# Causal attention with a decay bias, then a hard-swish MLP: a new hand order for the first eight head pairs and the first MLP block

## The chip, the cores and the metric

The kernel runs on one core of a Trainium2 chip. The metric is device time in microseconds (us) of one execution, the median over several. Engines are named as in the profile: PE (TensorE, matmul), PEld (its weight loads), DVE (VectorE), ACT (ScalarE), POOL (GpSimd), SP (SyncE, which here only issues transfers).

## The reference

There are 8 x 8 = 64 heads with 576 positions and 64 columns. Each head computes causal softmax attention with a bias that falls with the running sum of `max(s, 0)`. The 4608 x 512 result goes through an MLP with 2048 hidden columns.

```python
scores = scale * np.matmul(q, k.transpose(0, 1, 3, 2))
cum = np.cumsum(np.maximum(s, 0.0), axis=-1)
bias = -(cum[:, :, :, None] - cum[:, :, None, :])
scores = np.where(causal, -1000000000.0, scores + np.minimum(bias, 0.0))
attn = np.exp(scores - np.max(scores, axis=-1, keepdims=True))
attn = attn / (np.sum(attn, axis=-1, keepdims=True) + 1e-09)
x = np.matmul(attn, v)              # heads side by side: 4608 x 512
h = x @ w_in                        # 512 x 2048
g = h * np.clip(h + 3.0, 0.0, 6.0) / 6.0
out = g @ w_out                     # 2048 x 512
```

## The kernel before, in words

Heads are worked in 32 pairs. For a pair, `load_qk` and `load_v` bring q, k and v in float32 from HBM on SP's queue: two transfers for q and k, three for v. `cast_qk` (POOL) and `cast_v` (DVE for pairs 1 to 4, else POOL) make them float16. For the first ten pairs `transpose_group` turns q and k on TensorE in two groups, of five and four tiles of 128 x 128, and DVE copies the result into one of three slots of `qkT`; later pairs are transposed by DMA. Rows 64 to 127 of a slot hold the bias and a part of the causal mask: `mask_rows` fills them for each of the three slots, and for the first ten pairs `load_aug` writes the four rows of the running sum (three of it in float16 pieces for k, its negative for q) over the first of them. These rows are computed on DVE and ACT at the start, stored to HBM (`kaug_scratch`, `qaug_scratch`) and read back per pair; those of pair 0 are copied directly.

`scores_bank` computes one of four banks of a head's scores on TensorE, ACT takes the exponential into `Pm`, POOL zeroes what lies above the diagonal (the mask, L295). `attend` multiplies by the values (15 matmuls of 65 columns, the 65th gives the sum), and after the second head of a pair DVE takes the reciprocal and the product. `x_transpose` turns the pair's result into `xT`, on TensorE or by DMA.

The MLP works in nine blocks of 512 rows. `m1(n, f)` is four matmuls of 512 columns into a bank, then ACT (`trl`) and DVE (`gT`); there are 16 of them in a block. `m2(n, t4, part)` is four of the sixteen matmuls of an output tile; there are 16 parts in a block too. Such four matmuls are called a group here. Four pairs (one batch entry) give 576 rows of x, so block 0 needs the first four pairs. The weights w_in (two halves) and w_out (four parts) are loaded and cast by transfers that POOL issues, `load_w_in` and `load_w_out`.

PSUM has eight banks: tag M with two (`bank()`), S with three (scores, some transposes), Y with one (m2's output), O with two (attend).

There is no scheduler: the order on each engine is the order of the Python calls. `att_tasks(p)` gives the attention tasks of pair p with costs, `weave` puts MLP tasks between attention tasks in proportion to the costs, and `merged` mixes m1 of one block with m2 of the block before. In before, pairs 0 to 3 and the scores of pair 4 run first without MLP work (`att_of[0]`). Then m1 of block 0 and eight of its m2 parts are woven with pairs 4 to 8, m1 of block 1 with the other eight, two m1 to one m2, and from block 2 on 16 m1 with 16 m2 of the block before. SP's queue is in order, too: a transfer that waits holds all behind it.

The buffers that order the loads: `qkf` (float32 q and k) has three, v, `qkT` and `Pm` have three slots each.

Of the kernel before, what the change touches and what calls it, by code (L numbers as in the profile page):

```python
# [9 lines left out]
F32 = mybir.dt.float32  # L10
# [6 lines left out]
def kernel(  # L17
# [53 lines left out]
    kaug_dram = nc.dram_tensor("kaug_scratch", (3, NH * SEQ), F16, kind="Internal").ap()  # L71
    qaug_dram = nc.dram_tensor("qaug_scratch", (1, NH * SEQ), F16, kind="Internal").ap()
# [36 lines left out]
    kaug = work.tile([NH, 3, SEQ], F16, tag="s3", bufs=1)  # L109
    qaug = work.tile([NH, SEQ], F16, tag="s4", bufs=1)  # L110
# [8 lines left out]
    nc.gpsimd.memset(warm, 0.0)  # L119
# [16 lines left out]
    def load_qk(p, eng):  # L136
        b, h0 = (2 * p) // H, (2 * p) % H
        t = work.tile([128, NTR, 2, D], F32, tag="qkf", bufs=3, name=f"qkf{p}")
        for i, src in enumerate((q, k)):
            rows = src[b, h0:h0 + 2].rearrange("h s d -> (h s) d")  # L140
            eng.dma_start(  # L141
                out=t[:, :, i, :], in_=rows.rearrange("(t p) d -> p t d", p=128)
            )
        qk_f[p] = t
# [14 lines left out]
    def load_aug(p, eng):  # L159
        sl = p % NS  # L160
        c0 = p * W2
        eng.dma_start(out=kT[64:67, sl, 0:W2], in_=kaug_dram[:, c0:c0 + W2])
        eng.dma_start(out=qT[67:68, sl, 0:W2], in_=qaug_dram[:, c0:c0 + W2])
# [62 lines left out]
    def cast_v(p):  # L226
        sl = p % NS
        copy = nc.vector.tensor_copy if p in (1, 2, 3, 4) else nc.gpsimd.tensor_copy
        copy(out=v_h[:, sl, :, :, 0:D], in_=v_f[:, sl])  # L229
# [12 lines left out]
    def transpose_group(p, g):  # L242
        t0, t1 = ((0, 5), (5, 9))[g]
        n = (t1 - t0) * 128
        pT = half_bank(p < 5)
# [157 lines left out]
    def m1(n, f):  # L403
        if f == 0:
            gT[n] = work.tile([128, NF, 512], F16, tag="gT", bufs=2, name=f"gT{n}")
        ph = bank()
# [14 lines left out]
    def m2(n, t4, part):  # L421
        if part == 0:

            if (n, t4) in ((0, 1), (8, 1), (8, 3)):
                pouts[n, t4] = bank()
            else:
                pouts[n, t4] = psum.tile([128, 512], F32, tag="Y", name=f"po{n}_{t4}")
# [28 lines left out]
    load_v(0, nc.sync)  # L456
# [8 lines left out]
    for hh in range(2):  # L465
# [3 lines left out]
    nc.sync.dma_start(  # L469
        out=kaug_dram.rearrange("r (h t) -> h r t", h=NH), in_=kaug  # L470
    )
    nc.sync.dma_start(out=qaug_dram.rearrange("r (h t) -> h (r t)", h=NH), in_=qaug)
    mask_rows(1, nc.scalar.copy)
    load_v(1, nc.sync)
    load_aug(1, nc.sync)
    load_qk(2, nc.sync)
    load_v(2, nc.sync)

    weights_at = {1: [(load_w_in, 0)], 2: [(load_w_in, 1)]}
    pairs_at = {0: [3], 1: [4], 2: [], 3: [5], 4: [6], 5: [7, 8]}  # L480

    def att_tasks(p):
# [4 lines left out]
        def loads():  # L487
            if p + 2 < PTD:
                load_aug(p + 2, nc.sync)
            if p == 5:  # L490
                load_columns()
            for m in pairs_at.get(p, [p + 3] if p + 3 < NP else []):
                load_qk(m, nc.sync)
                load_v(m, nc.sync)
            if 4 < p < PTD - 1:
                cast_qk(p + 1)

        def casts():
            if more:
                cast_v(p + 1)  # L500
            if p + 2 <= 4:
                cast_qk(p + 2)
            if PTD <= p + 2 < NP:
                cast_columns(p + 2)
                transpose_dma(p + 2)
            for load, c in weights_at.get(p, []):
                load(c)

        def scores(hd):
            return [(lambda bi=bi: scores_bank(hd, bi), 400) for bi in range(4)]  # L510
# [5 lines left out]
        here = tr if p != 4 else [[], []]  # L516
        late = [(lambda: attend(2 * p - 1), 1200)] if p > 0 else []
        back = [(lambda: x_transpose(p - 1), 0 if by_dma(p - 1) else 640)] if p > 0 else []
        a = [(loads, 0)]
        if p <= PXD:  # L520
            a += scores(2 * p) + here[0] + late
            a += scores(2 * p + 1) + [(casts, 0)] + here[1] + back
        else:
            s0, s1 = scores(2 * p), scores(2 * p + 1)
            a = late + (back + a if by_dma(p - 1) else a + s0[:2] + back)
            a += (s0 if by_dma(p - 1) else s0[2:]) + here[0]
            a += s1 + [(casts, 0)] + here[1]
        if p == 6:
            a += [(decay_columns, 640)]
        if p == 7:  # L530
            a += [(copy_columns, 0)]
        c = [(lambda: attend(2 * p), 1200)]
        if p == 4:
            c += [(lambda: cast_qk(p + 1), 0)] + tr[0] + tr[1]
        return a, c

    att_of = [[]]
    for p in range(NP):
        a, c = att_tasks(p)
        att_of[-1] += a  # L540
        if p % 4 == 0 and p > 0:
# [41 lines left out]

    keep_warm(18)
# [3 lines left out]
    mask_rows(2, nc.vector.tensor_copy)  # L588
    cast_v(0)
    cast_qk(1)  # L590
    keep_warm(12)
    for task, _ in att_of[0]:
        task()

    first = [(task, 0.0 if f < 4 else 0.7) for f, (task, _) in enumerate(m1_tasks(0))]
    for c, f in enumerate((0, 2, 5, 8)):
        task, w = first[f]
        first[f] = ((lambda task=task, c=c: (task(), load_w_out(c))), w)  # L600
    m2_0 = m2_tasks(0)
    weave(att_of[1], first + m2_0[:8])
    weave(att_of[2], merged(m1_tasks(1), m2_0[8:], 2))
    for n in range(2, NBLK):
        weave(
            att_of[n + 1] if n + 1 < B else [],
            merged(m1_tasks(n), m2_tasks(n - 1), 4),
            0.85 if n + 1 == B - 1 else 1.0,
        )
    for task, _ in m2_tasks(NBLK - 1):  # L610
        task()
# [30 lines left out]
```

## Time and profile before

| | |
|---|---|
| median of 12 runs | 382.86 us (379.73 to 385.36) |
| the profiled execution | 382.8 us |
| its span, first to last instruction | 381.1 us |
| mean granted TensorE clock | 0.978 |
| PE busy | 354.8 us (93%) |
| ACT, DVE, POOL busy | 210.3, 190.9, 145.8 us |
| HBM over the span | 124 GB/s |

The page cuts the span into 40 slices of about 9.5 us; each digit is the busy share of an engine in tenths, or the granted clock, or the busy share of the 16 DMA engines. Rows of the timeline give the start in us from the span's start, the duration, engine, line, operation, output and inputs and the count; in brackets stands how long the engine was idle before it, and what ended that. Rows whose engine ends in q are a sequencer that issues a transfer; the duration is then that of the issue. Shares over the whole span say little here, since the first 90 us and the rest have different limits.

### The profile page before, as it was taken

The page shows a single profiled execution, that of the slowest core. Times are in us where ns is not written, and L with a number is a line of the kernel's source. Part 1 is how long each engine was busy: PE and PEld are TensorE (multiplying, and loading weights), DVE is VectorE, ACT ScalarE, POOL GpSimd, SP SyncE. Part 2 cuts the span into 40 slices and gives each one's busy share as a digit, 9 for nine tenths or more (in the row PEclk, how much of TensorE's full clock was granted, in tenths as well). Part 3 has the DMA queues.
Part 4 walks back from the last instruction along what each step waited for, and adds up shares of the span by engine and source line. Part 5 has one row for each costly group of instructions (what it writes and reads, how often), then busy time and mean ns, then how long its engine had stood idle before and what let it go on. Part 6 is the DMA issues. An engine that isn't in the chain of part 4 may idle for free.

```text
span 381.1 us, 7609 instructions
## 1 busy us (share of the span) xinstructions
PE 354.8 (93%) x2780; PEld 221.0 (58%) x2780; DVE 190.9 (50%) x329; ACT 210.3 (55%) x406; POOL 145.8 (38%) x375
## 2 busy tenths in 40 slices
PE   7775786899999999999999999999999999999995
PEld 2464554566666666666666666666666655555542
DVE  5545466676545444544454445444544544454531
ACT  4735556335776666666666666666566543443310
POOL 4365353445655555355545444444443200000000
PEclk9969799899999999999999999999999999999999
DMA  8699899945899999999998999989955101011011
GB/s 177 137 198 187 179 204 223 217 96 131 178 223 183 209 211 197 234 202 207 211 227 168 220 189 209 201 192 204 189 111 108 45 28 57 28 47 38 28 63 77
DMA packets 184621, 59.38 MB, mean 156 GB/s; under 512 B 177828, under 2 KB 178212, under 8 KB 184584
## 3 DMA queue, kind: packets, MB, share of 16 engines
q1 hardware_dynamic: 182536, 54.52, 67.5%
q0 software_dynamic: 1632, 4.19, 6.0%
q8 instruction: 22, 0.36, 0.4%
q10 hardware_dynamic: 416, 0.19, 0.2%
q14 instruction: 15, 0.12, 0.1%
HBM read 37.41 MB, written 9.73 MB: 124 GB/s over the span
## 4 chain that ended last, share of the span: by engine, by line
PE 83%; DMA 9%; ACT 2%; DVE 2%; issue 1%; POOL 1%; SPq 1%; POOLq 0%; ACTq 0%
PE bank L408 30%; PE po L430 29%; PE S L282 10%; PE O L331 7%; DMA qkf<-in_k_dram 5%; DMA qkT<-kaug_scratch 3%; PE bank L430 3%; ACT Pm L290 2%; POOL t L167 1%; DMA s_sb<-in_s_dram 1%; PE pT L369 1%; PE bank L450 1%; SPq L141 1%; DVE kaug L115 0%; PE pTm L238 0%
## 5 line engine op out<-in xcount | busy, mean ns | idle before, releaser
L416 ACT ACTIVATE trl<-bank,bias 128x512 f32<-128x512 f32 x144 | 99.4, 690 | 113.8 <-PE bank L408 112.8
L417 DVE SCALAR_TENSOR_TENSOR gT<-trl,bank 128x512 f16<-128x512 f32 x144 | 99.0, 687 | 122.7 <-ACT trl L416 122.7
L408 PE MATMUL bank<-xT,w_in 128*128 128x512 f16 x576 | 149.0, 385 | 1.3 <-DVE gT L417 1.3
L290 ACT ACTIVATE Pm<-S 128x384 f16<-128x384 f32 (+2 forms) x256 | 116.2, 505 | 33.4 <-PE S L282 32.1
L295 POOL TENSOR_SCALAR_AFFINE_SELECT Pm<-Pm 128x128 f16<-128x128 f16 (+2 forms) x256 | 78.6, 309 | 137.5 <-ACT Pm L290 127.7
L430 PE MATMUL po<-w_out_sb,gT 128*128 128x512 f16 x528 | 130.9, 379 | 0.0
L408 PEld LDWEIGHTS <-w_in 128*128 128x128 f16 x576 | 77.5, 146 | 31.6 <-issue 2.8
L430 PEld LDWEIGHTS <-gT 128*128 128x128 f16 x576 | 53.2, 98 | 51.3
L282 PE MATMUL S<-qkT 128*128 128x320 f16 (+4 forms) x448 | 71.0, 268 | 7.1 <-DMA qkT<-kaug_scratch 4.3
L282 PEld LDWEIGHTS <-qkT 128*128 128x128 f16 x448 | 42.0, 100 | 35.3 <-DMA qkT<-kaug_scratch 4.4
L331 PEld LDWEIGHTS <-Pm 128*128 128x128 f16 x960 | 39.6, 99 | 11.8 <-POOL Pm L295 0.4
L331 PE MATMUL O<-v_h,Pm 128*128 128x65 f16 x960 | 42.1, 196 | 0.3 <-POOL Pm L295 0.2
L343 DVE TENSOR_TENSOR xs<-O,r 128x640 f16<-128x640 f32 x32 | 26.4, 824 | 1.1
L213 POOL CAST xb<-qkf 128x1152 f16<-128x1152 f32 x22 | 25.2, 1147 | 0.0
L439 DVE TENSOR_SCALAR osb<-po 128x512 f32<-128x512 f32 x33 | 22.6, 684 | 5.0 <-PE po L430 5.0
L229 POOL CAST v_h<-v_f 128x640 f16<-128x640 f32 x28 | 20.6, 736 | 2.0 <-DMA v_f<-in_v_dram 2.0
L341 DVE RECIPROCAL r<-O 128x10 f32<-128x10 f32 x32 | 7.1, 220 | 25.9 <-PE O L331 25.8
L167 POOL CAST t<-qkf 128x1152 f16<-128x1152 f32 x10 | 11.7, 1172 | 13.9 <-DMA qkf<-in_k_dram 13.9
L238 PEld LDWEIGHTS <-t 128*128 128x128 f16 x90 | 6.5, 101 | 13.6 <-POOL t L167 9.2
L253 DVE COPY qkT<-pTm 64x640 f16<-64x640 f16 (+1 forms) x20 | 9.1, 454 | 8.4 <-PE pTm L238 8.1
L430 PE MATMUL bank<-w_out_sb,gT 128*128 128x512 f16 x48 | 11.3, 379 | 0.0
L253 DVE COPY qkT<-pT 64x640 f16<-64x640 f16 (+1 forms) x20 | 9.0, 452 | 4.4 <-PE pT L238 4.3
(40 smaller groups left out, 80.3 us busy)
## 6 DMA issues: line engine op xcount, KB each, us to landing
qkf<-in_q_dram SPq DMA_DIRECT2D x32, 288.0 KB, 3.6
qkf<-in_k_dram SPq DMA_DIRECT2D x32, 288.0 KB, 4.2
out_dram<-osb SPq DMA_DIRECT2D x36, 256.0 KB, 2.0
v_f<-in_v_dram SPq DMA_DIRECT2D x64, 128.0 KB, 3.8
w_in<-in_moe_w_in_dram POOLq DMA_DIRECT2D x2, 1024.0 KB, 11.6
w_out_sb<-in_moe_w_out_dram POOLq DMA_DIRECT2D x4, 512.0 KB, 8.5
v_f<-in_v_dram SPq DMA_DIRECT2D x32, 32.0 KB, 7.3
qkT<-xb SPq DMA_TRANSPOSE x22, 5.3
```

What stands on the lines that cost most here:

```text
L213: nc.gpsimd.tensor_copy(out=x.rearrange("p (i t) c -> p t i c", i=2)[:, :, :, 0:D], in_=qk_f.pop(p))
L229: copy(out=v_h[:, sl, :, :, 0:D], in_=v_f[:, sl])
L282: nc.tensor.matmul(out=S[:, c:c + hi - lo], lhsT=kT[:, sl, off + 128 * kt:off + 128 * (kt + 1)], rhs=qT[:, sl, off + lo:off + hi], start=( ...
L290: nc.scalar.activation(out=P[:, p0:p0 + n], in_=S[:, 0:n], func=AF.Exp, scale=0.125, bias=0.0)
L295: nc.gpsimd.affine_select(out=view, in_=view, pattern=pattern, compare_op=ALU.is_ge, fill=0.0, base=0, channel_multiplier=-1,)
L331: nc.tensor.matmul(out=O[:, hh, qt * VW:qt * VW + D + 1], lhsT=P[:, c:c + 128], rhs=v_h[:, sl, hh, kt, 0:D + 1], start=(qt == 0), stop=(qt ...
L343: nc.vector.tensor_tensor(out=xs.rearrange("p t h d -> p h t d"), in0=Ov[:, :, :, 0:D], in1=r.to_broadcast([128, 2, 5, D]), op=ALU.mult,)
L408: nc.tensor.matmul(out=ph, lhsT=w_in_t[f // 8][:, kc, f % 8, :], rhs=xT[:, kc, n * 512:(n + 1) * 512], start=(kc == 0), stop=(kc == KC - 1),)
L416: nc.scalar.activation(out=trl, in_=ph, func=AF.Relu, bias=bias3[:, 0:1], scale=1.0)
L417: nc.vector.scalar_tensor_tensor(out=gT[n][:, f, :], in0=trl, scalar=6.0, in1=ph, op0=ALU.min, op1=ALU.mult)
L430: nc.tensor.matmul(out=po, lhsT=gT[n][:, f, t4 * 128:(t4 + 1) * 128], rhs=w_out_sb[:, f, :], start=(f == 0), stop=(f == NF - 1),)
L439: nc.vector.tensor_scalar_mul(out=osb, in0=po, scalar1=1.0 / 6.0)
```

## The change

The bias rows of q and k go into one tile `aug` (with rows of ones written by POOL) and in two parts to HBM: eight heads first, by a transfer that POOL issues, then twelve heads (the others are not needed), by SP. `load_aug` is one transfer instead of two and brings four rows of both halves of the slot. The loads are placed by hand: q and k of pair 2 ahead of v of pair 0, v of pair 1 behind the bias rows of pairs 1 and 2. Pair 0's values are cast on DVE and multiplied behind the scores of head 2 instead of head 1. `mask_rows` of slot 1 moves from ACT to DVE. Pairs 0 to 3 run alone as before, but without the scores of pair 4; both halves of w_in are issued in pair 1. Then block 0's first m1 run on their own, on a bank of tag Y every third time, and pairs 4 to 7 follow, each as one sequence (`block0_tasks`): scores of both heads, loads and casts, both attends, the transposes of the next pair, x. All of block 0's m2 falls there. w_out is issued in two halves, the first behind the casts of pair 4, the second behind those of pair 5. In the later blocks, eight parts of a block's m2 follow its own m1, and the other eight run with the next block's m1, two m1 to one m2. In the last two blocks every second m1 uses a bank of tag S.

```diff
+    NA = 8
+    aug_drams = [
+        nc.dram_tensor("aug_scratch0", (2, 4, NA * SEQ), F16, kind="Internal").ap(),
+        nc.dram_tensor("aug_scratch1", (2, 4, (2 * PTD - NA) * SEQ), F16, kind="Internal").ap(),
+    ]
...
-    def load_qk(p, eng):
+    def load_qk(p, *engs):
...
     def load_aug(p, eng):
         sl = p % NS
-        c0 = p * W2
-        eng.dma_start(out=kT[64:67, sl, 0:W2], in_=kaug_dram[:, c0:c0 + W2])
-        eng.dma_start(out=qT[67:68, sl, 0:W2], in_=qaug_dram[:, c0:c0 + W2])
+        src, c0 = (aug_drams[0], p * W2) if 2 * p < NA else (aug_drams[1], p * W2 - NA * SEQ)
+        eng.dma_start(
+            out=qkT[64:68, sl, 0:2 * W2].rearrange("r (i c) -> r i c", i=2),
+            in_=src[:, :, c0:c0 + W2].rearrange("i r c -> r i c"),
+        )
...
     def cast_v(p):
-        copy = nc.vector.tensor_copy if p in (1, 2, 3, 4) else nc.gpsimd.tensor_copy
+        copy = nc.vector.tensor_copy if p < 4 else nc.gpsimd.tensor_copy
...
-        ph = bank()
+        if n >= B - 1 and f % 2:
+            ph = psum.tile([128, 512], F32, tag="S", bufs=3, name="bankS")
+        elif n == 0 and f % 3 == 2:
+            ph = psum.tile([128, 512], F32, tag="Y", name="bankY")
+        else:
+            ph = bank()
...
-            if (n, t4) in ((0, 1), (8, 1), (8, 3)):
+            if (t4 == 1 and n != 7) or (n, t4) in ((0, 3), (8, 3)):
                 pouts[n, t4] = bank()
...
+    def first_tasks(p):
+        def loads():
+            if p == 0:
+                load_qk(3, nc.sync)
+                load_v(2, nc.sync)
+            elif p == 1:
+                load_aug(3, nc.sync)
+                store_aug(1, NA, 2 * PTD, nc.sync)
+            else:
+                load_pair(p + 2)
+        def casts():
+            if p > 0:
+                cast_v(p)
+            if p == 1:
+                load_w_in(0)
+            if p < 2:
+                cast_qk(p + 2)
+            if p == 1:
+                load_w_in(1)
...
+        t = scores(2 * p)
+        if p == 1:
+            t += [(lambda: (cast_v(0), load_v(3, nc.sync)), 0), (lambda: attend(0), 1200)]
+        t += tr[0]
+        if p > 0:
+            t += [(lambda: attend(2 * p - 1), 1200)]
+        t += scores(2 * p + 1) + [(casts, 0)] + tr[1]
+        if p > 0:
+            t += [(lambda: x_transpose(p - 1), 640)]
+            t += [(lambda: attend(2 * p), 1200)]
+        return [(loads, 0)] + t
+
+    pause = [(lambda: None, 1000)]
+
+    def block0_tasks(p):
+        def ahead():
+            load_pair(p + 3)
+            cast_qk(p + 1)
+            cast_v(p + 1)
+            if p == 4:
+                load_w_out(2)
+                load_w_out(3)
...
+        return (
+            scores(2 * p)
+            + scores(2 * p + 1)
+            + [(ahead, 0), (lambda: attend(2 * p), 1200), (lambda: attend(2 * p + 1), 1200)]
+            + transposes(p + 1)
+            + [(lambda: x_transpose(p), 640)]
+            + pause
+        )
...
-    mask_rows(2, nc.vector.tensor_copy)
-    cast_v(0)
+    for sl in (1, 2):
+        mask_rows(sl, nc.vector.tensor_copy)
+    store_aug(0, 0, NA, nc.gpsimd)
+    for p in (1, 2):
+        load_aug(p, nc.sync)
+    load_v(1, nc.sync)
     cast_qk(1)
     keep_warm(12)
-    for task, _ in att_of[0]:
-        task()
...
+    for p in range(4):
+        run(first_tasks(p))
+    load_pair(6)
+    cast_qk(4)
+    cast_v(4)
+    load_w_out(0)
+    load_w_out(1)
+    keep_warm(4)
+    attend(7)
+    x_transpose(3)
+    m1_0, m2_0 = m1_tasks(0), m2_tasks(0)
+    run(m1_0[:8])
+    weave(transposes(4) + pause + pause + block0_tasks(4), m1_0[8:14])
+    weave(block0_tasks(5), m1_0[14:] + m2_0[:4])
+    weave(
+        block0_tasks(6) + [(decay_columns, 640), (copy_columns, 0)] + block0_tasks(7),
+        m2_0[4:],
+        0.85,
+    )
+    m2_of = {n: m2_tasks(n) for n in range(1, NBLK)}
+    weave(att_of[0], m1_tasks(1) + m2_of[1][:8])
+    for n in range(2, B - 1):
         weave(
-            att_of[n + 1] if n + 1 < B else [],
-            merged(m1_tasks(n), m2_tasks(n - 1), 4),
+            att_of[n - 1],
+            merged(m1_tasks(n), m2_of[n - 1][8:], 2) + m2_of[n][:8],
             0.85 if n + 1 == B - 1 else 1.0,
         )
-    for task, _ in m2_tasks(NBLK - 1):
-        task()
+    run(merged(m1_tasks(B - 1), m2_of[B - 2][8:], 2))
+    run(merged(m1_tasks(B), m2_of[B - 1], 4))
+    run(m2_tasks(NBLK - 1))
```

## The prediction, made before the result was known

> **What bounds the kernel now.** I read the slices of the page first, then a table of stretches, then TensorE's timeline in the bad stretch, then the queues behind its waits.
>
> ```profile
> PE   7775786899999999999999999999999999999995
> PEclk9969799899999999999999999999999999999999
> DMA  8699899945899999999998999989955101011011
> ```
>
> A slice is 9.5 us. TensorE is full from the tenth slice on; before that it is at 5 to 8 tenths, with a lowered clock three times. The DMA engines are full in the same slices.
>
> ```profile
> 8.00:43.80 35.80, 23.53 (x268) 17.74 (x269) 18.99 (x39) 18.89 (x42) 19.29 (x46) 0.81 0.91 180
> 43.80:91.70 47.90, 40.40 (x388) 26.43 (x386) 31.66 (x69) 24.62 (x50) 21.68 (x50) 0.96 0.83 177
> 91.70:122.00 30.30, 29.95 (x266) 20.01 (x263) 15.93 (x27) 21.80 (x46) 16.46 (x44) 1.00 0.92 183
> 122.00:305.00 183.00, 183.00 (x1521) 116.03 (x1520) 88.14 (x142) 116.72 (x233) 86.02 (x229) 1.00 0.91 186
> 305.00:376.70 71.70, 71.70 (x333) 38.54 (x330) 31.55 (x47) 24.06 (x35) 0.00 (x0) 1.00 0.12 45
> ```
>
> The columns are length, then busy PE, PEld, DVE, ACT, POOL, then clock, DMA share, GB/s. From 122 us on nothing can be won: 183.00 of 183.00. So the end is set by when TensorE gets through the first two rows.
>
> ```profile
> 21.47 0.71 PE L238 MATMUL pTm<-ident,t 128*128 128x128 f16 x5 [3.50 <-POOL t L167]
> 39.62 1.56 PE L282 MATMUL S<-qkT 128*128 128x256 f16 x7 [4.31 <-DMA qkT<-kaug_scratch]
> 46.36 1.89 PE L408 MATMUL bank<-xT,w_in 128*128 128x512 f16 x8 [0.63 <-DVE gT L417]
> 66.61 0.45 PE L238 MATMUL pT<-ident,t 128*128 128x128 f16 x5 [2.82 <-POOL t L167]
> ```
>
> These are the waits: for the cast of pair 2, for the bias rows of pair 4, for a bank (x8 is two groups in about 2.55 us, against 1.73 us below), for the cast of pair 6. The timelines of POOL, SP and DVE name the queues behind them:
>
> ```profile
> 20.27 1.14 POOL L167 CAST t<-qkf 128x1152 f16<-128x1152 f32 x1 [3.60 <-DMA qkf<-in_k_dram]
> ...
> 30.34 7.76 SPq L141 DMA_DIRECT2D qkf<-in_k_dram  x1
> ...
> 40.03 0.49 DVE L229 CAST v_h<-v_f 128x640 f16<-128x640 f32 x1 [5.71 <-DMA v_f<-in_v_dram]
> ```
>
> And in the chain that ended last:
>
> ```profile
> 28.25 11.31 DMA qkT<-kaug_scratch
> ...
> 305.91 1.73 PE bank L408 x8
> ```
>
> Pair 2's q and k come late since SP issues them at 15.5, behind v of pairs 0 and 1 and two stores. From 28 to 43 the two w_in halves fill the DMA engines and SP's loads crawl. The last line gives a price: a group of four MLP matmuls is 0.865 us.
>
> **The sum, to a common point.** Take E: eight pairs and MLP block 0 done, nothing of block 1. Before starts m1 of block 1 at 91.7, with eight m2 groups of block 0 owed (8 x 0.865 = 6.9) and the scores of pair 8 and transposes of pair 9 already done (1.4 + 0.5; a head's scores are 0.7 in the timeline, its values 0.47, nine transposes 0.5, x 0.28). E before is 91.7 + 6.9 - 1.9 = 96.7. What remains on TensorE after E is the same in both kernels.
>
> *Start to 16.4.* Nothing moves before the first scores at 12.7. SP loses v of pair 0 ahead of pair 1 (3.0 us of issue), v of pair 1 (1.9), two stores (1.2) and two bias loads (0.7) ahead of pair 2, so q and k of pair 2 go out at about 10 to 11 and land by 15 (median 4.2). The POOL cast follows the masks of heads 0 and 1 (to 16.7): ready at 17.9. The 3.50 wait goes, and with it the half clock after it (the clock's slice from 19 to 28.6 shows 6 tenths). Next late are the bias rows of pair 1. They now go over a store on POOL (issue as w_in's, 0.9, after the rows at 9.1; landing by the nearest row, the qaug store, 2.6) and then a load on SP, behind whose wait stand v of pair 1 and all of pair 3. The stores shrink from 288 KB to 8 and 12 heads of 9 KB (184 KB), the second one later on SP. Store landed 12.6, load issued 13.7, rows there at 16.2. Bounds: the row that waited 0.61 at 16.77 gives the same time; a store held up behind q, k and v could cost 4. I take 16.4. Hidden until then: the mask copies of slot 1, which move from ACT (2.2) to DVE (1.7), and pair 0's v cast, from POOL (1.25) to DVE (0.49); without the wait for the rows they would cost about 1. The POOL store ahead of pair 1's cast is hidden by 12 warming matmuls; uncovered it costs 0.9. The POOL memsets of the constant rows (about 2, scaled from warm's 0.52) lie in POOL's 4.9 idle before its first cast.
>
> *16.4 to the MLP.* The order within pairs 1 to 3 stays, and heads 4 to 7 in the trace run at 4.5 us a pair. Pair 1 has an extra attend and waits for masks: 5.4. Pair 2 has both w_in issues (0.9, 0.8) and a cast ahead of its masks on POOL: 5.0. Pair 3: 4.4. So 31.2; then four warming matmuls 0.9, attend(7), its reciprocal and product (1.04), x and its copy: m1 starts at 34.4. Before, m1 starts at 43.8, with scores and transposes of pair 4 (1.9) behind it: a lead of 43.8 - 34.4 - 1.9 = 7.5.
>
> *MLP block 0 with pairs 4 to 7.* Work: 32 groups 27.7, eight heads 9.4, five transposes 2.5, four x 1.1, decay 0.9: 41.6. Before needed 96.7 - 43.8 = 52.9 for 39.7 of it: 13.2 lost. After, by hand over the new order: groups 0 to 8 run at 0.865, since every third bank is Y (the two waits of 0.6 go); pair 4's block loses 3.9 (1.3 for the DVE copies of its transposes, 1.4 because two heads of scores stand together and ACT needs 8 x 0.42 for them, 1.0 for the last mask before attend(9)); pairs 5 and 6 lose 1.0 each; pair 7 loses 2.8, as the decay copies on DVE (3.1) hold all three S banks. Together 8.7. Covers: pair 4's cast ends at about 41, its transposes are due at 42.2; w_out parts 2 and 3 go out behind pair 5's casts at about 53 and land at 61 (median 8.5), m2 wants them at 60 to 61. Both fit by about 1 us; late, they cost 1:1. Behind POOL's wait for pair 5 stand the masks of head 10 and these two issues; behind the masks, attend(10) and all of m2. On SP each pair's loads now wait for the slot of the pair three before; its q and k buffers are free by then (pair 3's cast at 24), so this costs nothing unless POOL's casts slip. E after = 34.4 + 41.6 + 8.7 = 84.7. Gain 12.0.
>
> *Given back later.* Blocks 2 to 6 were woven as m1 and m2 one to one, without a wait. Now 16 m1 run with 8 m2, then 8 m2 alone. The row 91.70:122.00 had this 2:1 mix: 0.35 idle in 30 us. With runs of three m1 on two banks I take 0.6 a block, and block 1 has no m2 at all beside its m1: 3.0 in all (between 1 and 6). The second m2 tile on a bank of m1 instead of Y costs nothing, since it runs where no m1 does. The S banks for blocks 7 and 8 earn nothing: 305.91 already shows the full rate.
>
> Sum: 382.8 (the profiled execution's own time, the span of 381.1 and 1.7 around it, equal to the median) - 12.0 + 3.0 = 373.8, so 374.
>
> **A rule against the trace.** In the trace v of pair 4, issued at 26 to 28, arrives at 40.0, when w_in is nearly through: the software queue takes almost all. The Trainium skill (DMA: Bandwidth & Descriptors, Queues, rings and completion order) says that each engine alternates between queues packet by packet, a packet being some 9 to 17 descriptors. With SP's 256-byte rows that is 2.3 to 4.4 KB, an estimate of near half for SP. Then pair 4 would be early, but the second w_in half, out at 24.9, would land at 45 instead of 38, and group 8 at 41.3 would wait 4: 378. I follow the trace.
>
> **Rivals.**
> *Pair 3's v is caught behind w_in.* SP issues it at 22 to 24.6 and w_in's first packets start at about 24. If it lands with the end of w_in at 38, attend(6) slips from 31 to 38 and m1 starts near 42, with a cold clock (0.50 after such a pause): 12.0 falls to about 4, minus 3.0: 381 or 382. For: v of pair 4 in the trace. Against: without the big stores v of pair 3 is mostly through by 25, and is wanted at 30.7.
> *Slower: m1 in bunches make ACT the bound.* In blocks 2 to 6, an m1 with two score banks costs ACT 0.69 + 0.85 = 1.54, TensorE 0.86 + 0.36 = 1.22. If the bunched m1, 12 a block, each lose the 0.32, five blocks lose 19: 382.8 - 12 + 19 = 390. It decides from 2.4 a block, 0.2 per m1. For: ACT is busier in 91.70:122.00 (72%). Against: that row lost only 0.35.
> *The lead is larger.* If the pairs interleave as smoothly as 80 to 90 us does, with 3 lost instead of 8.7 by E: 368; with nothing given back, 365.
>
> **How the numbers follow.** As forecast, 369 to 379: 0.56. Larger lead: 0.08. Pair 3's v: 0.20, half of it still faster, 0.07 the same, 0.03 slower. ACT bound: 0.16, of which 0.03 within the bound. About 0.5% (1.9 us) can be told from no change. Faster 0.56 + 0.08 + 0.10 = 0.74, same 0.10, slower 0.03 + 0.13 = 0.16. The range from 364 to 386 leaves out the best tail and most of the ACT case.
>
> **What would show it.** Right: no wait for a cast between 17 and 22; clock at 1.00 through the first pairs; m1 from about 34; block 1 from about 85 instead of 97; small waits for gT in blocks 2 to 6. Wrong: m1 after 40 with DVE's v cast waiting for a load; POOL casts of pair 5 waiting and m2 starting after 65; TensorE idle over 2 us a block after 122; scores of pair 1 waiting for bias rows past 18.

## The result, and the profile after

| | before | changed kernel |
|---|---|---|
| median | 383.36 us (49 runs, 379.4 to 386.17) | 386.41 us (12 runs, 376.4 to 387.92) |
| the profiled execution | 382.8 us, span 381.1 | 384.62 us, span 382.8 |
| mean granted TensorE clock | 0.978 | 0.987 |

The twelve executions fall into two groups with nothing between: two at 376.4 and 376.89 us, ten from 383.76 to 387.92 us. The comparison that gives a ratio of 0.9833 [0.9786, 0.9879] counts only the executions near 376; the other group belongs to the program, as the experiments show. A typical execution of the changed kernel is thus slower than before (386.41 / 383.36 = 1.008, a quotient of medians, without an interval), and now and then one is 1.7% faster. The profiled execution is of the upper group.

The page's slices, 9.6 us each here:

```profile
PE   6773788989999999999999999999999999999995
PEclk9988899999999999999999999999999999999999
DMA  8699998645699999999999889989996210001012
```

The fourth slice, from 28.7 to 38.3 us, has dropped to 3 tenths, the emptiest of all, and the clock stands at 8 tenths around it. The seventh and eighth are fuller than before. The same stretches as before (length, then busy PE, PEld, DVE, ACT, POOL, then clock, DMA share, GB/s):

```profile
8.00:43.80 35.80, 21.83 (x249) 15.34 (x250) 18.16 (x37) 13.42 (x32) 17.91 (x42) 0.86 0.89 172
43.80:91.70 47.90, 42.79 (x391) 27.47 (x390) 30.39 (x68) 24.52 (x48) 20.00 (x45) 1.00 0.74 158
91.70:122.00 30.30, 29.67 (x262) 19.84 (x259) 17.36 (x30) 23.21 (x48) 15.95 (x45) 1.00 0.92 187
122.00:305.00 183.00, 181.66 (x1501) 115.15 (x1500) 86.24 (x142) 118.08 (x233) 88.05 (x232) 1.00 0.95 192
```

The first row did not gain, it lost: 21.83 busy against 23.53. TensorE's timeline says where:

```profile
17.43 1.33 PE L291 MATMUL S<-qkT 128*128 128x256 f16 x7 [1.67 <-DMA qkT<-aug_scratch]
...
39.05 0.98 PE L340 MATMUL O<-v_h,Pm 128*128 128x65 f16 x15 [6.81 <-DVE v_h L238]
39.84 1.90 PE L465 MATMUL bank<-warm 128*128 128x512 f16 x4
...
43.74 1.95 PE L423 MATMUL bank<-xT,w_in 128*128 128x512 f16 x8
54.14 0.56 PE L291 MATMUL S<-qkT 128*128 128x256 f16 x4 [1.03 <-DVE qkT L262]
...
56.72 0.65 PE L291 MATMUL S<-qkT 128*128 128x192 f16 x4 [0.69 <-ACT Pm L299]
...
59.73 0.49 PE L340 MATMUL O<-v_h,Pm 128*128 128x65 f16 x10 [0.71 <-POOL Pm L304]
...
93.55 1.03 PE L423 MATMUL bank<-xT,w_in 128*128 128x512 f16 x4
```

Pair 1's scores wait 1.67 us for its bias rows, some later than forecast. Then TensorE waits 6.81 us for the values of pair 3, warms at half clock (granted 0.50 from 39.84 to 41.74, four matmuls in 1.90 us), and m1 of block 0 starts at 43.74, where it started before. The three rows from 54 to 60 are pair 4's forecast losses, in their forecast order. The row at 93.55 is point E. Behind the 6.81, on DVE, SP and POOL of the same execution:

```profile
38.50 0.49 DVE L238 CAST v_h<-v_f 128x640 f16<-128x640 f32 x1 [6.78 <-DMA v_f<-in_v_dram]
...
24.54 0.61 SPq L161 DMA_DIRECT2D v_f<-in_v_dram  x1
25.25 0.66 SPq L148 DMA_DIRECT2D qkf<-in_q_dram  x1
25.95 10.11 SPq L148 DMA_DIRECT2D qkf<-in_k_dram  x1
...
23.36 0.79 POOL L392 DMA_DIRECT2D w_in<-in_moe_w_in_dram  x1
```

And one line of the chain that ended last:

```profile
24.54 13.84 DMA v_f<-in_v_dram
```

The last of the three transfers of pair 3's v, 32 KB, goes out at 24.54, 1.18 us behind the first half of w_in (23.36). It lands at 38.38, 13.84 us later, when w_in is nearly through. This is the rival "pair 3's v is caught behind w_in". From there on the kernel goes as forecast, only late. No m2 waits for w_out.

The single DMA packets of the same trace, counted in the order of issue, show how it is caught. All three transfers of v together are 1152 packets of 256 bytes. When the first packet of w_in starts, at 25.01, 141 of them are done: it is most of v that is caught, not its last 32 KB alone. From 28 to 37 us w_in's queue moves 790 packets and SP's 748, about one for one. But w_in's are of 2 KB, so w_in gets 1.62 MB and SP 0.19 MB.

### The profile page after: what moved, and what is told of

It is laid out like the page before. It is cut to its first block, busy times and chain, and to the rows that moved or that the text cites. A ratio compares the mean times of both kernels' runs of the same rounds, so it can differ in the third digit from the quotient of the medians.

```text
span 382.8 us, 7607 instructions
## 1 busy us (share of the span) xinstructions
PE 355.1 (93%) x2784; PEld 220.1 (57%) x2784; DVE 190.1 (50%) x331; ACT 209.3 (55%) x404; POOL 148.3 (39%) x378
## 4 chain that ended last, share of the span: by engine, by line
PE 78%; DMA 9%; DVE 4%; ACT 4%; SPq 2%; issue 2%; POOL 1%; ACTq 0%; POOLq 0%; DVEq 0%
PE bank L423 25%; PE po L445 22%; PE S L291 9%; PE bank L445 8%; PE O L340 6%; DMA v_f<-in_v_dram 4%; PE bankS L423 4%; ACT Pm L299 2%; DMA qkT<-xb 2%; DMA qkf<-in_k_dram 1%; ACT trl L431 1%; DVE gT L432 1%; DVE qkT L262 1%; SPq L148 1%; DMA qkT<-aug 1%
## 5 line engine op out<-in xcount | busy, mean ns | idle before, releaser
L432 DVE SCALAR_TENSOR_TENSOR gT<-trl,bank 128x512 f16<-128x512 f32 x123 | 84.5, 687 | 101.9 <-ACT trl L431 101.6
L431 ACT ACTIVATE trl<-bank,bias 128x512 f32<-128x512 f32 x123 | 85.1, 692 | 85.4 <-PE bank L423 83.6
L423 PE MATMUL bank<-xT,w_in 128*128 128x512 f16 x492 | 126.4, 382 | 0.7
L445 PE MATMUL po<-w_out_sb,gT 128*128 128x512 f16 x416 | 104.3, 379 | 0.0
L423 PEld LDWEIGHTS <-w_in 128*128 128x128 f16 x576 | 78.4, 146 | 33.4 <-issue 2.4
L445 PE MATMUL bank<-w_out_sb,gT 128*128 128x512 f16 x160 | 39.4, 379 | 0.0
L454 DVE TENSOR_SCALAR osb<-po 128x512 f32<-128x512 f32 x26 | 17.9, 688 | 15.2 <-PE po L445 14.9
L454 DVE TENSOR_SCALAR osb<-bank 128x512 f32<-128x512 f32 x10 | 6.9, 691 | 26.0 <-PE bank L445 26.0
L423 PE MATMUL bankS<-xT,w_in 128*128 128x512 f16 x64 | 16.4, 379 | 0.0
L431 ACT ACTIVATE trl<-bankS,bias 128x512 f32<-128x512 f32 x16 | 11.0, 687 | 8.0 <-PE bankS L423 8.0
```

What stands on the lines that cost most here:

```text
L423: nc.tensor.matmul(out=ph, lhsT=w_in_t[f // 8][:, kc, f % 8, :], rhs=xT[:, kc, n * 512:(n + 1) * 512], start=(kc == 0), stop=(kc == KC - 1),)
L431: nc.scalar.activation(out=trl, in_=ph, func=AF.Relu, bias=bias3[:, 0:1], scale=1.0)
L432: nc.vector.scalar_tensor_tensor(out=gT[n][:, f, :], in0=trl, scalar=6.0, in1=ph, op0=ALU.min, op1=ALU.mult)
L445: nc.tensor.matmul(out=po, lhsT=gT[n][:, f, t4 * 128:(t4 + 1) * 128], rhs=w_out_sb[:, f, :], start=(f == 0), stop=(f == NF - 1),)
L454: nc.vector.tensor_scalar_mul(out=osb, in0=po, scalar1=1.0 / 6.0)
```

## The experiments

Each ratio is to the kernel before on the same chip, with its 95% interval; the medians of before there were 381.46 us (for e1 to e4), 381.64 (e5 to e8) and 381.92 (e9 to e12). The group sizes in the expectations say "3 in 13" for the executions near 376; it is 2 in 12 timed ones, and the profiled one lies in the other group.

**Pair 3's v surely ahead of w_in** (e1_v3_ahead). SP sends v ahead of the second store; POOL sends w_in behind pair 3's cast:

```diff
             elif p == 1:
                 load_aug(3, nc.sync)
-                store_aug(1, NA, 2 * PTD, nc.sync)
...
-            if p == 1:
-                load_w_in(0)
             if p < 2:
                 cast_qk(p + 2)
             if p == 1:
+                load_w_in(0)
                 load_w_in(1)
...
-            t += [(lambda: (cast_v(0), load_v(3, nc.sync)), 0), (lambda: attend(0), 1200)]
+            t += [
+                (lambda: (cast_v(0), load_v(3, nc.sync), store_aug(1, NA, 2 * PTD, nc.sync)), 0),
+                (lambda: attend(0), 1200),
+            ]
```

> The changed kernel, but the store of the second bias part stands behind v of pair 3 on SP instead of ahead of it, and the first w_in half is issued behind the cast of pair 3 instead of ahead of it. Theory (a race on the DMA engines: the last of the three v transfers of pair 3 goes out at 24.5 us, w_in's first packets flow from about 25; if v loses, it arrives at 38 and attend(6) waits 6.8 us): v of pair 3 lands before 28, no wait over 1 us at attend(6), m1 of block 0 starts at 35 to 36 and the times lie in one group at 375 to 378, none at 384 to 388. Rival (the two groups of times of the changed kernel, 376 and 384 to 388, come from the clock of the chip and not from the program): both groups stay. Rival 2 (attend(6) waits for something else too): the wait stays under another name.

Measured: 375.81 us (375.15 to 377.7, 6 runs), 0.9874 [0.9838, 0.991]. One group. Its SP and POOL timelines:

```profile
23.35 0.61 SPq L161 DMA_DIRECT2D v_f<-in_v_dram  x1
...
24.35 1.53 POOL L392 DMA_DIRECT2D w_in<-in_moe_w_in_dram  x2
```

Now v leads by 1.0 us, all its packets are done (25.36) before w_in's first one starts (26.47), its cast on DVE waits for nothing, and the upper group is gone.

**Pair 3's v surely behind w_in** (e2_v3_behind). The opposite, to make the loss happen every time:

```diff
             else:
-                load_pair(p + 2)
+                if p == 2:
+                    load_qk(4, nc.sync)
+                    load_v(3, nc.sync)
+                    load_v(4, nc.sync)
+                    load_aug(4, nc.sync)
+                else:
+                    load_pair(p + 2)
...
-            t += [(lambda: (cast_v(0), load_v(3, nc.sync)), 0), (lambda: attend(0), 1200)]
+            t += [(lambda: cast_v(0), 0), (lambda: attend(0), 1200)]
```

> The changed kernel with the opposite edit: v of pair 3 is issued behind q and k of pair 4, so that it always stands behind the start of w_in. Theory of the race: v of pair 3 lands near 38 to 40 in every execution, m1 starts at 44 or later, all times at 385 to 389 (the upper group of the changed kernel or 1 to 2 us over it), none near 376. Rival (chip clock): two groups as before, some times near 376.

Measured: 388.16 us (385.75 to 389.71, 6 runs), 1.0189 [1.0148, 1.0231], all in the upper group or up to 1.8 us above it. From its waits (what waited, for what, then us in total, times, longest):

```profile
PE O L340 <- DVE v_h L238: 9.6, 1, 9.6
```

One wait of 9.6 us for the same cast. With e1 this shows the mechanism from both sides: order alone moves the time by 12 us.

**Which of e1's two edits is needed?** Only the store moved (e6_store_behind_v):

```diff
             elif p == 1:
                 load_aug(3, nc.sync)
-                store_aug(1, NA, 2 * PTD, nc.sync)
...
-            t += [(lambda: (cast_v(0), load_v(3, nc.sync)), 0), (lambda: attend(0), 1200)]
+            t += [
+                (lambda: (cast_v(0), load_v(3, nc.sync), store_aug(1, NA, 2 * PTD, nc.sync)), 0),
+                (lambda: attend(0), 1200),
+            ]
```

> The changed kernel with one transfer moved: the store of the second bias part on SP behind v of pair 3 instead of ahead of it. w_in stays where the change put it, ahead of pair 3's cast. v then goes out about 0.4 us earlier. Theory of the race: 0.4 us is of the size of the margin, so the share of executions near 376 rises from 3 in 13, perhaps to half or more; if both groups appear, they still lie at 376 and 385 with nothing between. Rival (the order of SP alone decides): all near 376. Rival (w_in's place alone decides): as the changed kernel.

Measured: 385.55, 375.49, 383.81, 385.19, 383.77 and 376.3 us; the ratio of the two low ones is 0.9866 [0.9805, 0.9926]. Two groups again, nothing between; two low ones in six against two in twelve tell no change in the share. The profiled one (span 383.8) is of the upper group; POOL, SP and DVE in it:

```profile
21.91 0.79 POOL L392 DMA_DIRECT2D w_in<-in_moe_w_in_dram  x1
...
23.78 0.77 SPq L161 DMA_DIRECT2D v_f<-in_v_dram  x1
...
37.82 0.49 DVE L238 CAST v_h<-v_f 128x640 f16<-128x640 f32 x1 [7.26 <-DMA v_f<-in_v_dram]
```

v goes out earlier, but so did w_in in this execution: it leads by 1.87 us, its first packet starts at 23.43 with none of v's done, and v is caught.

Only w_in moved (e10_w_in_behind_cast):

```diff
             if p > 0:
                 cast_v(p)
-            if p == 1:
-                load_w_in(0)
             if p < 2:
                 cast_qk(p + 2)
             if p == 1:
+                load_w_in(0)
                 load_w_in(1)
```

> The changed kernel with the other half of e1's edit alone: the first w_in half is issued behind the cast of pair 3 instead of ahead of it, 1.2 us later; SP's order stays as the change has it. Theory of the race (the margin is a fraction of a microsecond, and what counts is when w_in's packets start against v's last transfer): all or nearly all executions near 376, since 1.2 us is more than the 0.4 us of e6, which left two groups. Rival (SP's store ahead of v is needed too): two groups.

Measured: 375.43 us (374.92 to 376.41, 6 runs), 0.9832 [0.9798, 0.9865]. One group, with the lowest median of the study (e1 and its repeat lie within 0.5 us), from two lines put behind one. Its page:

```profile
PE   6778879999999999999999999999999999999995
PEclk9999999999999999999999999999999999999999
```

Its stretches:

```profile
8.00:43.80 35.80, 28.45 (x297) 19.58 (x297) 24.25 (x47) 19.53 (x41) 19.24 (x43) 1.00 0.91 177
43.80:91.70 47.90, 42.73 (x413) 27.38 (x412) 29.72 (x69) 24.01 (x51) 21.74 (x53) 1.00 0.92 194
91.70:122.00 30.30, 29.72 (x283) 19.63 (x282) 14.49 (x25) 21.70 (x45) 19.85 (x50) 1.00 0.93 187
122.00:305.00 183.00, 182.16 (x1485) 115.02 (x1484) 88.19 (x144) 117.99 (x232) 83.78 (x224) 1.00 0.89 183
```

And SP, POOL, DVE and TensorE in its timeline:

```profile
24.19 0.61 SPq L161 DMA_DIRECT2D v_f<-in_v_dram  x1
...
24.00 1.53 POOL L392 DMA_DIRECT2D w_in<-in_moe_w_in_dram  x2
...
30.63 0.56 DVE L238 CAST v_h<-v_f 128x640 f16<-128x640 f32 x1
...
34.67 1.95 PE L423 MATMUL bank<-xT,w_in 128*128 128x512 f16 x8
...
84.48 1.03 PE L423 MATMUL bank<-xT,w_in 128*128 128x512 f16 x4
```

w_in's first issue leads by only 0.19 us, and v lands in time. So the lead at which v is caught lies between 0.2 and 1.2 us (the upper-group execution of the changed kernel). In packets: 899 of v's 1152 are done here when w_in's first one starts, at 25.52, where it was 141 there. m1 starts at 34.67, nine microseconds earlier than in that execution, the clock stays at 1.00, and E is at 84.48.

**The weave of the later blocks, alone in the kernel before** (e4_before_two_to_one): eight parts of a block's m2 behind its own m1, the other eight with the next block two to one, and the bank choices of the change for these blocks.

```diff
-    weave(att_of[2], merged(m1_tasks(1), m2_0[8:], 2))
-    for n in range(2, NBLK):
+    m2_of = {n: m2_tasks(n) for n in range(1, NBLK)}
+    weave(att_of[2], merged(m1_tasks(1), m2_0[8:], 2) + m2_of[1][:8])
+    for n in range(2, B - 1):
         weave(
-            att_of[n + 1] if n + 1 < B else [],
-            merged(m1_tasks(n), m2_tasks(n - 1), 4),
+            att_of[n + 1],
+            merged(m1_tasks(n), m2_of[n - 1][8:], 2) + m2_of[n][:8],
             0.85 if n + 1 == B - 1 else 1.0,
         )
```

> The kernel before with only the later part of the change: eight m2 parts of each block behind its own m1 and two m1 to one m2 for the rest, from block 1 on, with the bank choices that go with it (bank of tag M for the second m2 tile, of tag S for every second m1 of the last two blocks). Theory of the give-back: 3 to 5 us slower than before, 386 to 388. Rival (this order costs nothing; what the changed kernel loses after block 0 is the price of its front): within 1 us of before. Third view (the S banks and the shorter lag between m1 and m2 help at the end): 1 to 2 us faster.

Measured: 382.81 us (380.54 to 385.1, 12 runs), 1.0051 [1.002, 1.0081]: by the ratio 1.9 us slower, between 0.8 and 3.1. The order does cost, but less than the 3 to 5 of the theory. Its long stretch:

```profile
122.00:305.00 183.00, 182.44 (x1494) 115.76 (x1492) 86.04 (x141) 119.72 (x235) 86.75 (x230) 1.00 0.90 187
```

0.56 idle where before had none, and no engine near its limit: ACT is busy 119.72 of 183. The rival that ACT becomes the bound is out.

**The weave put back into e1** (e3_one_to_one). Block 1 is m1 alone with attention, from block 2 on 16 m1 with 16 m2 one to one, with the bank choice of before for the m2 tiles of blocks 1 to 7:

```diff
-    weave(att_of[0], m1_tasks(1) + m2_of[1][:8])
+    weave(att_of[0], m1_tasks(1))
     for n in range(2, B - 1):
         weave(
             att_of[n - 1],
-            merged(m1_tasks(n), m2_of[n - 1][8:], 2) + m2_of[n][:8],
+            merged(m1_tasks(n), m2_of[n - 1], 4),
             0.85 if n + 1 == B - 1 else 1.0,
         )
```

> As e1, with the later blocks woven as in the kernel before: block 1's m1 alone, then from block 2 on 16 m1 with 16 m2 of the block before, one to one. Theory (the changed order of the later blocks gives back 4 to 5 us: with the profiled changed kernel 289.3 us pass from the start of block 1 to the end, against 284.4 worked out for the kernel before): 3 to 5 us below e1, that is 371 to 374, and no idle TensorE between 122 and 305. Rival (the give-back comes from the transfers, which the earlier front only shifts): within 1 us of e1.

Measured: 381.77 us (380.11 to 382.16, 12 runs), 1.0005 [0.998, 1.003]. A miss: 6 us slower than e1. Its stretches:

```profile
85.00:122.00 37.00, 29.25 (x271) 19.98 (x270) 17.43 (x30) 26.59 (x56) 19.97 (x54) 0.95 0.90 182
122.00:305.00 183.00, 183.00 (x1521) 116.01 (x1519) 87.48 (x141) 116.25 (x232) 85.72 (x228) 1.00 0.92 183
```

And its waits:

```profile
PE S L291 <- ACT Pm L299: 6.9, 16, 0.7
PE S L291 <- DMA qkT<-xb: 3.5, 2, 3.0
```

The long stretch is full again, as the edit wanted, but block 1, with 16 groups of MLP work beside its attention where there were 24, runs the attention ahead of what feeds it: TensorE is idle 7.75 us of 37, waiting for ACT's exponentials and for q and k that DMA transposes.

**A milder form of the same** (e11_later_one_to_one): block 1 as in the change, block 2 takes the eight owed parts and leaves none of its own ahead, blocks 3 to 6 are one to one, with the bank choice of before for the m2 tiles of blocks 2 to 7.

```diff
     weave(att_of[0], m1_tasks(1) + m2_of[1][:8])
-    for n in range(2, B - 1):
+    weave(att_of[1], merged(m1_tasks(2), m2_of[1][8:], 2))
+    for n in range(3, B - 1):
         weave(
             att_of[n - 1],
-            merged(m1_tasks(n), m2_of[n - 1][8:], 2) + m2_of[n][:8],
+            merged(m1_tasks(n), m2_of[n - 1], 4),
             0.85 if n + 1 == B - 1 else 1.0,
         )
```

> As e1, with block 2 at two m1 to one m2 without the eight parts behind it, and blocks 3 to 6 one to one as in the kernel before. e4 puts the 2:1 order at about 1.9 us for blocks 1 to 6 (1.0051 of before). Theory: 1 to 2 us faster than e1, 374 to 375. Rival (as e3 showed in block 1, attention then runs ahead of its transposes by DMA and TensorE waits there): slower than e1 by up to 2.

Measured: 377.02 us (376.5 to 377.77, 6 runs), 0.9874 [0.9838, 0.991]. From its waits:

```profile
PE S L291 <- DMA qkT<-xb: 2.3, 2, 1.2
```

e1 once more, on the same chip (e12_e1_again):

> The same kernel as e1, beside e10 and e11 on the same chip. The race theory: again one group, 375 to 378, and none near 385.

Measured: 375.92 us (374.7 to 380.31, the others up to 377.13, 6 runs), 0.9855 [0.9806, 0.9905]. The one-to-one weave is no better here, if anything 1.1 us worse: with eight groups of MLP work fewer in block 2 the attention again gets ahead of the DMA transposes (the two waits begin at 123 and 140 us). In the changed kernel the eight m2 parts behind each m1 are also what keeps the attention back.

**A part of block 0's m2 left for block 1** (e8_spread, on e1): four parts less among pairs 6 and 7, four more in block 1, and their tile on Y instead of an m1 bank.

```diff
         block0_tasks(6) + [(decay_columns, 640), (copy_columns, 0)] + block0_tasks(7),
-        m2_0[4:],
+        m2_0[4:12],
         0.85,
...
-    weave(att_of[0], m1_tasks(1) + m2_of[1][:8])
+    m1_1 = m1_tasks(1)
+    first = []
+    for i in range(4):
+        first += m1_1[4 * i:4 * i + 2] + m2_0[12 + i:13 + i] + m1_1[4 * i + 2:4 * i + 4]
+    weave(att_of[0], first + m2_of[1][:8])
```

> As e1, with four of block 0's m2 parts left over for block 1, one to every four of its m1, where e1's profile is at its least even after block 0 (TensorE idle 0.64 of 37 us in the table, and about 2 more hidden between matmuls, from 85 to 122). A try at a better kernel: 0.5 to 1.5 us faster than e1 (375.8), 374.5 to 375.3, if the bunched m1 of block 1 are what loses there; no faster, or slower by up to 1, if pairs 6 and 7 need the four parts to fill their own waits.

Measured: 377.66 us (376.05 to 381.42, 12 runs), 0.9929 [0.989, 0.9968]. Probably worse than e1 (0.9874 [0.9838, 0.991] on its chip); three of the twelve, at 380.69 to 381.42, are unexplained. From the waits:

```profile
PE S L291 <- DVE dec L216: 1.4, 1, 1.4
```

The scores of pair 7 wait 1.4 us for the S banks that the decay copies on DVE hold, where e10 shows no wait over 0.7 us. That pairs 6 and 7 miss the four parts more than block 1 wants them fits this, but is not shown.

**Bank Y taken from block 0** (e5_no_y_bank, on e1):

```diff
-        elif n == 0 and f % 3 == 2:
-            ph = psum.tile([128, 512], F32, tag="Y", name="bankY")
```

> As e1 (v of pair 3 ahead), with block 0's m1 on the two banks of tag M alone. The prediction counted groups 0 to 8 at 0.865 us because every third uses bank Y; before shows two groups in 2.55 us on two banks. Theory: each pair of groups in the first nine loses about 0.8, together 3, of which pair 4's cast (ready at 43.9 in e1's profile, its transposes due at about 44) hides nothing: 2 to 3.5 us slower than e1 (375.8), 378 to 379. Rival (the second w_in half and pair 4's cast set the pace there, not the banks): within 1 us of e1.

Measured: 378.29 us (378.09 to 381.85, 10 runs), 0.9943 [0.9912, 0.9974]. 2.5 us slower than e1's 375.81 (2.6 by the ratios, each on its own chip). Its waits:

```profile
PE bank L421 <- DVE gT L430: 2.5, 4, 0.6
```

Four waits of 0.6 us come back where m1 runs on its own. The third bank is worth 2.5 us.

**The early order of loads, alone in the kernel before** (e9_before_early_loads): q and k of pair 2, then v of pair 0, ahead of the stores; pair 0's values cast on DVE right ahead of `attend(0)`.

```diff
     load_qk(0, nc.sync)
-    load_v(0, nc.sync)
     load_qk(1, nc.sync)
...
+    load_qk(2, nc.sync)
+    load_v(0, nc.sync)
     nc.sync.dma_start(
         out=kaug_dram.rearrange("r (h t) -> h r t", h=NH), in_=kaug
...
     load_v(1, nc.sync)
     load_aug(1, nc.sync)
-    load_qk(2, nc.sync)
     load_v(2, nc.sync)
...
+        if p == 0:
+            c = [(lambda: (cast_v(0), load_v(3, nc.sync), attend(0)), 1200)]
```

> The kernel before with only the first part of the new load order, as e7 meant it: q and k of pair 2 ahead of v of pair 0 and of the two bias stores; v of pair 0 cast on DVE just ahead of its use, and v of pair 3 loaded behind that. Theory (the wait moves on): the wait of 3.5 us for pair 2's cast goes, but w_in is issued earlier too and catches the bias rows and v of pair 4 again; 0 to 1.5 us faster than before. Rival (each early wait counts in full): 3 to 4.5 us faster. Third view, from e7, where attend(0) waited 11.2 us for v of pair 3 and m1 of block 0 still began only 1.7 us later than before: the early stage has so much slack behind w_in that nothing changes, within 0.5 us.

Measured: 382.74 us (379.39 to 384.85, 12 runs), 1.0007 [0.9975, 1.004]: nothing. TensorE in its profiled execution:

```profile
20.63 0.98 PE L331 MATMUL O<-v_h,Pm 128*128 128x65 f16 x15 [5.12 <-DVE v_h L229]
...
39.07 1.95 PE L408 MATMUL bank<-xT,w_in 128*128 128x512 f16 x8
...
49.04 0.71 PE L238 MATMUL pT<-ident,t 128*128 128x128 f16 x5 [3.38 <-POOL t L167]
```

Even with a new wait of 5.12 us for v of pair 0, m1 starts at 39.07, 4.7 us earlier than before. The lead is lost at 49: pair 5's transposes wait for its cast, and POOL is behind, at

```profile
46.07 0.72 POOL L229 CAST v_h<-v_f 128x640 f16<-128x640 f32 x1 [6.26 <-DMA v_f<-in_v_dram]
```

waiting for another v that crawls beside w_in. That execution was the fastest of the twelve, so some of the lead lived on in it (379.39), but not in the median. An earlier form of it (e7_before_early_loads) let the load of pair 3's v take the slot before pair 0's values were cast, so pair 0 is multiplied with pair 3's values and waits for them:

```diff
+        if p == 0:
+            c = [(lambda: (cast_v(0), attend(0)), 1200)]
```

> The kernel before with only the first part of the new load order: q and k of pair 2 ahead of v of pair 0 and of the two bias stores, v of pair 0 cast on DVE just ahead of its use. Theory (the wait moves on): the wait of 3.5 us for pair 2's cast goes, but w_in is issued earlier too, the bias rows of pair 4 and v of pair 4 are still caught behind it, and TensorE waits longer than 4.3 us for them before MLP block 0: 0 to 1.5 us faster than before. Rival (each early wait counts in full): 3 to 4.5 us faster.

Measured: 386.11 us (385.2 to 388.09, 6 runs), 1.0141 [1.01, 1.0182]. It answers little about the loads, but gives a price:

```profile
26.85 0.98 PE L331 MATMUL O<-v_h,Pm 128*128 128x65 f16 x15 [11.17 <-DVE v_h L229]
```

A wait of 11.17 us at this place, the earlier loads included, costs 4.5 us (386.11 - 381.64) in the end.

## Why the prediction was right or wrong

*What decided most executions: wrong in its weight.* The mechanism of the first rival is what the profiled execution shows and, by e1, e2 and e10, what made ten executions of twelve slow; it had a chance of 0.20. The failed step is its "against: without the big stores v of pair 3 is mostly through by 25, and is wanted at 30.7". It was not through: at 25.0 us 139 of its 1152 packets were done in the profiled execution, and 364 in e10's. One store of 108 KB still stood right ahead of v on SP (issued at 22.80, its packets ran from 23.60 to 25.34), v's three transfers went out from 23.20 to 24.54, and a cast waits for the last of them. The prediction had the two times within a microsecond ("22 to 24.6", "about 24") and should have seen that an order that close is open, execution by execution; it is no single time but two. That two executions came near the forecast of 374 is then luck as much as foresight: the typical one, 386.41, lies above the stated range of 364 to 386. The 381 or 382 for this rival was too low as well: the profiled execution took 384.6. Its m1 began at 43.74, not near 42, since v landed at 38.38 and the warming and first work behind it ran with a cold clock (0.50 from 39.05 to 41.60). The rest is in the two terms below.

*The first 34 us: right.* Where v is in time (e10), m1 starts at 34.67; forecast 34.4. The bias rows of pair 1 come at 16.87 in e10 and 17.43 in the changed kernel, forecast 16.4, within its bounds. The wait of 3.50 us for pair 2's cast is gone, and in e10 the clock stays at 1.00.

*Block 0 with pairs 4 to 7: right.* The stalls were put at 8.7 us. In e10 the intervals from one matmul's start to the next, beyond the median of their width, sum to 8.4 us from 34.67 to 84.48. Pair 4's three losses of 1.3, 1.4 and 1.0 show as waits of 1.03, 0.69 and 0.71 in the changed kernel's timeline; in e10 the losses there sum to 3.1 with the smaller ones, for 3.9 (the three named come to 3.7). E came at 84.48; forecast 84.7. Bank Y was worth 2.5 (e5). w_out was in time, as forecast: no wait of m2 for it in either profile.

*E in before: the count was too high by a group and one head's values.* The sum held "eight m2 groups of block 0 owed" at 91.7. The groups of before, for the window up to there:

```profile
L430 PE MATMUL po<-w_out_sb,gT 128*128 128x512 f16 x20 | 5.1, 380 | 0.0
...
L430 PE MATMUL bank<-w_out_sb,gT 128*128 128x512 f16 x16 | 4.1, 379 | 0.0
```

And its timeline just ahead of 91.7:

```profile
90.40 1.03 PE L430 MATMUL po<-w_out_sb,gT 128*128 128x512 f16 x4
91.26 0.64 PE L331 MATMUL O<-v_h,Pm 128*128 128x65 f16 x15
```

20 + 16 = 36 matmuls are nine groups, not eight: `merged` begins with an m2, so one of the second eight had run (at 90.40). Seven were owed. The values of head 16, of the ninth pair, had run too (at 91.26; 240 such matmuls, for 16 heads, came before), 0.5 us that the sum left out. E in before is 91.7 + 6.1 - 1.9 - 0.5 = 95.4, not 96.7. The gain by E is 95.4 - 84.48 = 10.9 us for e10, for a forecast of 12.0, and 95.4 - 93.55 = 1.9 us in the profiled execution of the changed kernel.

*The give-back: right in size.* From E to the end of the span before takes 381.1 - 95.4 = 285.7 us, e10 373.2 - 84.48 = 288.7, the changed kernel 382.8 - 93.55 = 289.3. So 3.0 and 3.6 us are given back; forecast 3.0 (1 to 6). (The expectations of the experiments, written with the old count, speak of a larger one.) Where it lies, worked out from the trace: for every matmul from E on (in before from 91.7, in e3, e4 and e11 from block 1's first m1), the time to the next one's start, less the median of that width in before, summed by what the next one is.

| kernel | next is m1 | next is scores | other | sum, us |
|---|---|---|---|---|
| before | 1.5 | 0.4 | 0.0 | 1.9 |
| changed, upper group | 3.8 | 1.6 | 0.5 | 5.9 |
| e10 | 3.8 | 1.0 | 0.6 | 5.3 |
| e4: before with the new weave | 3.7 | 0.1 | -0.6 | 3.1 |
| e11: blocks 3 to 6 one to one | 2.0 | 3.3 | 1.1 | 6.4 |
| e3: from block 2 one to one | 2.3 | 9.0 | 0.9 | 12.1 |

The sums less that of before are 4.0 and 3.4. That is 0.4 more than what is given back, since the end, from the last matmul's start on, is 0.4 us shorter (4.4 for 4.8). The larger part, 2.3 us, is m1, as forecast for bunched m1 on two banks, and e4 shows it without the rest of the change (2.1, unrounded). It is the bank that m1 waits for: of e10's m1 losses 2.7 us stand at matmuls that start within 0.12 us of the end of a DVE `gT`, the step that frees a bank; in before it is 0.15. The table also says why putting the weave back did not pay: e11 and e3 win back 1.5 to 1.8 us on m1 and lose 2.3 and 8 on scores.

*The sum, mended.* For an execution in which v is in time: 382.8 - 10.9 + 3.0 = 374.9; for the other kind: 382.8 - 1.9 + 3.6 = 384.5. These agree with the profiled executions of e10 (374.92) and of the changed kernel (384.62) by construction, since the give-back was taken from their spans: they show how the time divides and confirm nothing. What can be set against the forecast of 374 is e10's median of 375.43 and the changed kernel's two at 376.4 and 376.89. Against the forecast, e10's terms are 1.1 us short in the gain, which is nearly all the miscount of E in before (1.3), and right in the give-back.

*The other rivals.* ACT as the bound fell (e4: 1.9 us in all, where it needed 2.4 a block). The larger lead did not come: 8.4 of stalls, not 3.

*The rule against the trace: no conflict.* The prediction set the trace (the software queue takes nearly all) against the near half for SP that it estimated from the Trainium skill (DMA: Bandwidth & Descriptors, Queues, rings and completion order). The counts agree with that page's turns between queues: 790 packets of w_in against 748 of SP from 28 to 37 us. (A packet of the trace is a single row here, one of the page a bundle of descriptors; equal counts fit turns of equal length.) It was the estimate that was wrong. It took the bytes of SP's turn, 2.3 to 4.4 KB, and left out that w_in's packets are eight times as large. With as many packets of 2 KB against those of 256 bytes SP's share is a ninth, an estimate from the page's rule and the trace's sizes; measured are 0.19 of 1.81 MB, 11%. So the reading of the trace pointed the right way, and it was applied to pair 4 only, not to pair 3's v.

*Open.* No profile shows one of the changed kernel's two low executions; that v was in time there is concluded from e1, e2 and e10. What makes the issue times differ from execution to execution was not tried, nor where between 0.2 and 1.2 us the lead decides. How e9 loses its lead was read in one execution only, its fastest. And e1's edits leave one execution in twelve at 380.31 (e1 and e12 together), which no profile caught.

## What to carry to other kernels

Where a small transfer is wanted soon and a large one is about to start on another queue, let a dependency or the order on one engine decide which goes first (here w_in behind a cast that waits for loads: all six executions at 374.92 to 376.41 us), and look at the spread of the executions, not the median alone, when two issues lie within a microsecond. Time a load by its last part, and ask how much of it is done when the first packet of a rival load starts. A share of the DMA engines worked out from turns needs the packet sizes of both sides. Count owed work instruction by instruction from the groups' view; a group and one head's values were 1.3 us of the error here.

## What the runs showed of the hardware

- A transfer of 32 KB on SP's queue, issued 1.18 us behind a w_in half on POOL's queue, took 13.84 us; in e10, with a w_in lead of 0.19 us, it was there in time. While both flowed, the queues moved about as many packets (790 and 748 in 9 us), and the bytes went as the packet sizes, 2 KB and 256 bytes. SP was held 10.11 us in its next large issue. Whether v was caught moved m1 by 9.1 us and the time by 8 (the changed kernel's profiled execution less its two low ones) to 10 us (the median of its ten high ones less the same).
- A stretch can be called full and still lose time. In the stretch from 122 to 305 us e10 has 182.16 busy of 183.00, and from E on TensorE's waits sum to 0.7 us by the waits' view, yet start-to-start intervals show 3.4 us more than before. Of the 3.7 us of m1 losses in e10, 2.0 lie inside the modelled end of the matmul before, where the view has no idle time.
- A long pause cost more than its length: after the 6.81 us the four warming matmuls took 1.90 us at a granted clock of 0.50; in e10, without the pause, the same four took 1.02.
